# A hashed-attention kernel with a channel mix behind it: one step of the mix placed two slots later, a weight scaling placed two slots later, a flag read placed elsewhere in the program

## The chip, the cores and the metric

The kernel runs on one core of one Trainium2 chip. Its metric is the device time of one execution, in microseconds (us). Before the change it took 281.64 us (median of 3 runs, 281.24 to 282.11). A core has a matrix engine (PE, whose weight loads are listed apart as PEld), a vector engine (DVE), an activation engine (ACT), a general engine (POOL, also called GpSimd) and a sequencer that here only issues transfers (SP). Each engine works through its own instructions in program order, and waits on semaphores for the others.

## The reference

Four batches of eight heads, 768 positions and 64 features go through an attention in which a query sees only the keys of its own hash bucket. The result, 768 x 512 per batch, goes through a "channel mix":

```
mask   = q_bucket[:, :, :, None] == k_bucket[:, :, None, :]      # 6 sign bits of q@proj, k@proj
attn   = softmax(where(mask, q @ k.T / 8, -1e9));  x = attn @ v
x_prev = x shifted by one position (zero ahead of the first)
xk     = mu_k * x + (1 - mu_k) * x_prev
xr     = mu_r * x + (1 - mu_r) * x_prev
out    = sigmoid(xr @ w_r) * (relu(xk @ w_k) ** 2 @ w_v)
```

## The kernel before, in words

Two heads make a pair, four pairs make a batch, so there are 16 pairs. All of `fast()` is written in a hand-made order: the order of the Python calls is the order of the instructions on each engine. Its main loop counts slots G. Twelve slots make a turn, n = G // 12, and s = G % 12 is the slot within it. In one slot the PE makes the scores of one block of 128 keys against all 768 queries of one head (`score`, matmuls at L325), ACT takes their exponential (L332), and two slots behind it (LAG = 2) the PE multiplies them with the values (`pv`, L352). A head takes six slots, so a turn takes one pair.

Around this stand, in fixed slots of turn n:

- s = 1 (3 in turn 0), `bits`: the PE projects the queries and keys of pair n+1 (L287), DVE takes the sign bits (L291), and SP writes them in 8 small transfers (L297).
- s = 3, `turn_out`: the PE transposes the attention result of pair n-1 (L378), DVE copies it to `xt` (L379), and a copy of 127 columns (L384) completes the shifted version. That last copy is made by POOL for the first three pairs of a batch and by DVE for the fourth (t == NPB - 1).
- s = 4, `mix(..., 0)`: DVE makes df = x - x_prev (L394), then xk = mu_k * df (L398) and adds x_prev (L405). The L394 waits for the copy of L384. In turns 5 to 15, `mix(..., 1)` makes xr at s = 8 (in the first batch at odd slots of turns 4 and 5).
- s = 5, 7, 9, 11, `turn`: the PE transposes queries and keys of pair n+2 (L269), DVE copies them out of their bank (L272 for queries, L274 for keys); half goes into the operand of the scores by POOL (L277), half by DVE (L278).
- s = 6, 10, `values`: POOL converts and sums the values of pair n+1 (L305 to L315).
- s = 8, 10, `norm`: ACT squares queries and keys with a sum (L256), for pairs 6 to 15.

The matmul results lie in single banks. "A" to "D" are four of them. The attention result of a head (`oo`) takes bank A or C in turns 0 to 3, by head, and always bank A from turn 4 on (`oo_bank`, L599). The bank is free again when DVE has read it: `rc` (L363) and `ob` (L364), issued after the sixth `pv` of a head, in slot 7 for the first head of a turn. The first `pv` of the next head begins with the matmul of L343 into the same bank. It stands at the end of slot 8, after that slot's other PE work. So from turn 4 on L343 of slot 8 waits for the `ob` of slot 7.

The three products of the channel mix are a queue of items (`ffn_items`, matmuls at L424: kp, rp, vp). From turn 4 on they are issued by a credit of work per slot and fill the PE; batch b is worked on while the attention of batch b+1 runs. Their results take banks C and D in turn. A kp is read by DVE (L449) or ACT (L447) and squared by DVE (L455), an rp by ACT (L464), a vp by DVE (L487), after which SP stores the result (L491).

The weights w_v are loaded by SP in four parts (`load_wv`, L544) at s = 0 and 2 of turns 1 and 2 into two staging buffers, and POOL scales each part to bf16 (L550) eight slots after its load was issued (`later(8, ...)`). `later(k, f)` runs f at the head of the slot k after. POOL also issues the transfers of w_k and w_r (L537), w_r at s = 10 of turns 1 and 2.

At the end a flag says whether the scores stayed in a safe range (`check_bound`, L671). `nc.values_load` makes every engine read it into a register (L842), and a branch (L843) skips a slower general version. It stands after `fast()`, outside of the hand-made order; in the built program SP reads the flag ahead of its last four stores, the other engines after their last instruction.

```
                    if s == 3 and n >= 1:
                        turn_out(n - 1, mb)
                    if s == 4 and n >= 1:
                        mix((n - 1) // NPB, (n - 1) % NPB, 0)
```

Of the kernel before, what the change touches and what calls it, by code (L numbers as in the profile page):

```python
# [29 lines left out]
def kernel(  # L30
# [13 lines left out]
    nc = tc.nc  # L44
    B, H, S, D = q.shape
# [3 lines left out]
    NC_ = S // P  # L49
# [3 lines left out]
    NPB = H // 2  # L53
# [23 lines left out]
    flag = consts.tile([1, 1], INT32, name="flag")  # L77
# [90 lines left out]
    def fast():  # L168
        with ExitStack() as fx:
# [44 lines left out]
            def later(k, fn):  # L214
                due.append((clock[0] + k, len(due), fn))

            def run_due():
                ready = sorted(x[:2] for x in due if x[0] <= clock[0])
                for key in ready:
                    fn = next(x for x in due if x[:2] == key)  # L220
                    due.remove(fn)
                    fn[2]()
# [4 lines left out]
            def load_qk(n, split=False, eng=nc.sync):  # L227
                b, t = divmod(n, NPB)
                tag = f"qk{n}" if n < NKEEP else f"qk{n % 3 - 3}"
                tl = nat.tile([P, 2, 2, S // 2], FP32, name=f"qk{n}", tag=tag)  # L230
                nats[n] = tl
                if split:
                    for j in range(2):
                        for (side, i, src), e in zip(SIDES, (nc.sync, nc.scalar)):
                            e.dma_start(out=tl[:, i, j, :], in_=natural(src, b, 2 * t + j))
                else:
                    for side, i, src in SIDES:
                        eng.dma_start(
                            out=tl[:, i, :, :],
                            in_=src[b, 2 * t : 2 * t + 2].rearrange(  # L240
                                "j (p c) d -> p j (c d)", c=NC_
                            ),
                        )
# [143 lines left out]
            mx = {}  # L387
# [28 lines left out]
            def group(shape, name, mms, done):  # L416

                box = {}

                def item(i, lhs, rhs):  # L420
                    def u():
                        if i == 0:
                            box["t"] = ffbank(shape, name)
                        nc.tensor.matmul(  # L424
                            box["t"], lhs(), rhs(), start=(i == 0), stop=(i == len(mms) - 1)
                        )
                        if i == len(mms) - 1:
                            done(box["t"])

                    return u  # L430

                return [item(i, *m) for i, m in enumerate(mms)]
# [44 lines left out]
            def v_items(b, c, parts=1):  # L477
                sp, cc = divmod(c, 3)
                kcols = slice(cc * P, (cc + 1) * P)
                items = []  # L480
                w = DM // parts
                for pt_ in range(parts):
                    ms = slice(pt_ * w, (pt_ + 1) * w)

                    def done(vp, ms=ms, pt_=pt_):
                        os_ = osp.tile([P, w], FP32, name=f"os{b}_{c}_{pt_}", tag="os")
                        nc.vector.scalar_tensor_tensor(  # L487
                            out=os_, in0=mx["th", b, c][:, ms], scalar=1.0, in1=vp,
                            op0=ALU.add, op1=ALU.mult,
                        )  # L490
                        nc.sync.dma_start(  # L491
                            out=out[b].rearrange("(p c) m -> c p m", c=NC_)[c][:, ms], in_=os_
                        )

                    mms = [
                        (
                            lambda fc=fc: mx["k2", b, sp, fc][:, kcols],
                            lambda fc=fc, ms=ms: wv_sb[:, fc, ms],
                        )
                        for fc in range(NFC)  # L500
                    ]
                    items += [
                        (0.215 / parts, u)
                        for u in group([P, w], f"vp{b}_{c}_{pt_}", mms, done)
                    ]
                return items
# [35 lines left out]
            def load_wv(c0):  # L542
                st = stg.tile([P, 2, DM], FP32, name=f"wvs{c0}", tag="stg")
                nc.sync.dma_start(  # L544
                    out=st,
                    in_=moe_w_v[c0 * P : (c0 + 2) * P, :].rearrange("(c p) f -> p c f", p=P),
                )
                later(
                    8,
                    lambda: nc.gpsimd.tensor_scalar(  # L550
                        out=wv_sb[:, c0 : c0 + 2, :], in0=st, scalar1=0.5, scalar2=1.0,
                        op0=ALU.mult, op1=ALU.mult,
                    ),
                )
# [44 lines left out]
            def oo_bank(n, j):  # L599
                return "AC"[j] if n < NPB else "A"  # L600

            def misc_bank(n, s):
                return "BD"[(s // 2) % 2] if n < NPB else "B"

            for G in range(nslots + LAG):
                clock[0] = G
                n, s = divmod(G, 12)
                live = G < nslots
                run_due()

                if live and s == (5 if n == 0 else 3):
                    if n + 3 < NPAIRS:
                        load_qk(n + 3)
                    if n + 2 < NPAIRS:
                        load_v(n + 2)
                w = weights.get(n, {}).get(s)
                if w:
                    if w[0] == "v":
                        load_wv(w[1])
                    else:  # L620
                        load_w(*w)
                old = chunks[G - LAG] if G >= LAG else None
                first = old is not None and old[2] == 0
                if live:
                    score(*chunks[G])
                if old and not first:
                    pv(*old, oo_bank(*old[:2]))
                rate = 25.9 / (NPB * 12 + (3 if n >= NPAIRS - NPB else 0))
                ffn(rate / 2)
                mb = misc_bank(n, s)  # L630
                if live:
                    if n == 0:
                        if s in (0, 1):
                            turn(1, s, 1, "BD"[s])
                    if n == 1 and s == 0:
                        mups = bank(mb, [P, 2 * NDC], FP32, "mups")
                        nc.tensor.transpose(mups, mu_rows, ident32[0 : 2 * NDC, 0 : 2 * NDC])
                        nc.vector.tensor_copy(mu_sb, mups)
                    if s == (3 if n == 0 else 1) and n + 1 < NPAIRS:
                        bits(n + 1, (0, 1), mb)  # L640
                    if s == 3 and n >= 1:
                        turn_out(n - 1, mb)
                    if s == 4 and n >= 1:
                        mix((n - 1) // NPB, (n - 1) % NPB, 0)

                    if n in (NPB, NPB + 1) and G - NPB * 12 in (7, 9, 11, 13):
                        mix(0, (G - NPB * 12 - 7) // 2, 1)
                    if n > NPB and s == 8:
                        mix((n - 1) // NPB, (n - 1) % NPB, 1)
                    if s in (5, 7, 9, 11) and n + 2 < NPAIRS:  # L650
                        x = (s - 5) // 2
                        turn(n + 2, x % 2, x // 2, mb)
                    if s in (6, 10) and n + 1 < NPAIRS:
                        values(n + 1, s // 10)
                    if s in (8, 10) and NKEEP <= n + 1 < NPAIRS:
                        norm(n + 1, (s - 8) // 2)
                ffn(rate / 2)
                if old and first:
                    pv(*old, oo_bank(*old[:2]))
                if live and n >= NPB and n % NPB == 0 and s == MIXSLOT - 1:  # L660
                    queue.extend(ffn_items(n // NPB - 1))
# [16 lines left out]
            def step():  # L678
                nonlocal G
                clock[0] = G  # L680
                run_due()
                G += 1
# [14 lines left out]
            while queue:  # L697
# [7 lines left out]
                if x == 4 * NKEEP + 8:  # L705
                    check_bound()
            step()

    def general():

# [127 lines left out]
        )  # L838

    with tc.manual_schedule():  # L840
        fast()
    ok = nc.values_load(flag[0:1, 0:1], min_val=0, max_val=1)  # L842
    with tc.If(ok == 0, preferred_fallthrough_block=True):  # L843
        general()

# [29 lines left out]
```

## Time and profile before

| | |
|---|---|
| median of 3 runs | 281.64 us |
| profiled execution, its own time | 281.45 us |
| its span, first to last instruction | 279.6 us |
| mean granted PE clock | 0.988 |
| busy: PE, DVE, ACT, POOL | 94%, 71%, 77%, 41% |
| chain that ended last: PE, ACT, DVE, DMA | 66%, 9%, 8%, 7% |
| time moved by transfers | mean 107 GB/s |
| DVE L394 waited for POOL L384 | 6.9 us in 10 waits, longest 3.5 |
| POOL L550 waited for a transfer of w_v | 1.8 us, once |

A profile line such as "41.23 0.56 DVE L394 TENSOR_TENSOR df<-xt" gives the start, the duration, the engine, the line of the kernel and what is written from what. A bracket behind it is the time that the engine sat idle just before it, and what ended this. Durations of neighbours on one engine overlap by up to 0.1 us, so costs are better taken from start to start. The ends of matmuls are modelled.

### The profile page before, as it was taken

Reading aid. Unit: us, or ns where it says so; the run is one execution under the profiler, and the core shown is the slowest. Engines: PE = TensorE matmul, PEld = TensorE weight load, DVE = VectorE, ACT = ScalarE, POOL = GpSimd, SP = SyncE. Lnnn points to the kernel's source line nnn. Section 1 sums busy time; section 2 is a strip of 40 time slices with the busy share of each in tenths; the row PEclk is TensorE's granted clock in tenths of the full one; section 3 lists DMA queues with packets and bytes.
Section 4 is the critical chain, followed back from the end, with each engine's and each line's share of the span. In section 5 each row is a group of like instructions: output and inputs, shape, how many; then the busy total and the mean of one; then the engine's idle time right before and its main releaser. Section 6 shows DMA issues by size and latency. Waiting matters only on the chain.

```text
span 279.6 us, 6894 instructions
## 1 busy us (share of the span) xinstructions
PE 262.2 (94%) x2530; PEld 165.4 (59%) x2561; DVE 198.6 (71%) x438; ACT 215.0 (77%) x318; POOL 113.3 (41%) x300
## 2 busy tenths in 40 slices
PE   7999997899999999999999999999999889989991
PEld 5466765666565665656565765656565556545540
DVE  3766839879997866769698766769698835576541
ACT  2199995898799896878989896878998898449800
POOL 5885667665554350714455260715444600000000
PEclk9999997999999999999999999999999999999997
DMA  7459597253213050726122040815220001320042
GB/s 231 167 115 208 179 328 248 43 173 101 77 59 117 6 172 4 218 110 191 59 69 108 14 164 7 272 53 166 84 60 4 5 2 39 114 76 2 0 151 86
DMA packets 19896, 29.95 MB, mean 107 GB/s; under 512 B 2184, under 2 KB 15056, under 8 KB 19856
## 3 DMA queue, kind: packets, MB, share of 16 engines
q1 hardware_dynamic: 17928, 25.89, 27.9%
q0 software_dynamic: 1536, 3.15, 5.3%
q8 instruction: 22, 0.36, 0.5%
q10 hardware_dynamic: 392, 0.40, 0.5%
q14 instruction: 18, 0.15, 0.2%
HBM read 24.12 MB, written 6.29 MB: 109 GB/s over the span
## 4 chain that ended last, share of the span: by engine, by line
PE 66%; ACT 9%; DVE 8%; DMA 7%; issue 3%; SPq 3%; POOL 2%; ACTq 0%; DVEq 0%
PE sc L325 15%; PE vp L424 13%; PE kp L424 12%; PE oo L352 8%; ACT pt L332 6%; PE rp L424 5%; DMA wvs<-in_moe_w_v_dram 4%; PE bb L287 4%; PE tpq L269 3%; PE tpk L269 2%; SPq L297 2%; PE ot L378 2%; ACT sq L256 2%; PE oo L343 1%; DMA aq<-sg 1%
## 5 line engine op out<-in xcount | busy, mean ns | idle before, releaser
L332 ACT ACTIVATE pt<-sc,expb 128x768 bf16<-128x768 f32 x192 | 166.5, 904 | 39.4 <-PE sc L325 38.1
L325 PE MATMUL sc<-aq,ak 70*128 70x384 bf16 x384 | 94.9, 328 | 3.2 <-ACT pt L332 0.8
L352 PEld LDWEIGHTS <-pt 128*128 128x128 bf16 x1152 | 61.1, 98 | 26.6 <-issue 0.8
L352 PE MATMUL oo<-va,pt 128*128 128x65 bf16 x1152 | 66.9, 194 | 0.0
L424 PE MATMUL kp<-xk,wk_sb 128*128 128x384 bf16 x256 | 57.7, 325 | 0.8 <-DVE os L487 0.8
L325 PEld LDWEIGHTS <-ak 70*128 70x128 bf16 x384 | 34.9, 98 | 29.3 <-issue 9.1
L424 PE MATMUL vp<-wv_sb,k 128*128 128x512 bf16 (+1 forms) x186 | 50.3, 370 | 0.4 <-issue 0.2
L277 POOL CAST aq<-tq 64x384 bf16<-64x384 f32 x32 | 21.1, 658 | 63.3 <-DVE tq L272 63.3
L455 DVE TENSOR_TENSOR k<-kr 128x384 bf16<-128x384 bf16 x64 | 29.0, 459 | 15.5 <-ACT kr L447 14.3
L424 PEld LDWEIGHTS <-wk_sb 128*128 128x128 bf16 x256 | 22.2, 97 | 13.3 <-issue 4.2
L256 ACT ACTIVATE sq<-qk 128x768 bf16<-128x768 f32 x32 | 27.1, 847 | 0.1
L424 PE MATMUL rp<-wr_sb,xr 128*128 128x512 bf16 x79 | 24.9, 379 | 1.2 <-DVE kr L449 0.8
L424 PEld LDWEIGHTS <-k 128*128 128x128 bf16 x200 | 17.5, 97 | 12.0 <-issue 2.7
L447 ACT ACTIVATE kr<-kp 128x384 bf16<-128x384 f32 x36 | 17.7, 491 | 7.4 <-PE kp L424 7.4
L487 DVE SCALAR_TENSOR_TENSOR os<-th,vp 128x512 f32<-128x512 bf16 (+1 forms) x25 | 16.5, 663 | 9.0 <-PE vp L424 8.9
L384 POOL COPY xt<-xt 128x127 bf16<-128x127 bf16 x12 | 3.6, 302 | 46.4 <-DVE xt L379 46.4
L311 POOL TENSOR_TENSOR s<-vf 128x192 f32<-128x192 f32 x32 | 20.8, 650 | 0.0
L277 POOL CAST ak<-tk 64x384 bf16<-64x384 f32 x32 | 19.3, 602 | 2.4 <-DVE tk L274 2.4
L274 DVE TENSOR_SCALAR tk<-tpk 128x384 f32<-128x384 f32 x32 | 17.6, 550 | 3.4 <-PE tpk L269 3.3
L272 DVE COPY tq<-tpq 128x384 f32<-128x384 f32 x32 | 17.7, 552 | 2.1 <-PE tpq L269 2.0
L269 PE MATMUL tpq<-ident,qk 128*128 128x128 f32 x96 | 16.9, 287 | 2.4 <-DVE tq L272 1.7
L379 DVE COPY xt<-ot 128x768 bf16<-128x768 bf16 x16 | 8.9, 558 | 14.3 <-PE ot L378 14.2
(60 smaller groups left out, 320.0 us busy)
## 6 DMA issues: line engine op xcount, KB each, us to landing
vf<-in_v_dram SPq DMA_DIRECT2D x16, 384.0 KB
out_dram<-os SPq DMA_DIRECT2D x23, 256.0 KB
qk<-in_q_dram SPq DMA_DIRECT2D x13, 384.0 KB
qk<-in_k_dram SPq DMA_DIRECT2D x13, 384.0 KB
wvs<-in_moe_w_v_dram SPq DMA_DIRECT2D x4, 512.0 KB
aq<-sg SPq DMA_DIRECT2D x64, 4.5 KB
wk_sb<-in_moe_w_k_dram POOLq DMA_DIRECT2D x2, 512.0 KB, 5.4
ak<-sg SPq DMA_DIRECT2D x62, 4.5 KB
```

What stands on the lines that cost most here:

```text
L256: nc.scalar.activation(junk, nats[n][:, i].rearrange("p j f -> p (j f)"), AF.Square, accum_out=nrm[:, i, n : n + 1],)
L269: nc.tensor.transpose(tp[:, cols], nats[n][:, i, j, cols], ident32)
L272: nc.vector.tensor_copy(dst, tp)
L274: nc.vector.tensor_scalar(out=dst, in0=tp, scalar1=ALPHA, scalar2=None, op0=ALU.mult)
L277: nc.gpsimd.tensor_copy(au[side, j][0:D, 0:HALF], dst[0:D, :])
L311: nc.gpsimd.tensor_add(s3, vf[:, 0 : 3 * D], vf[:, 3 * D : 6 * D])
L325: nc.tensor.matmul(sc[:, sp, 0:HALF], au["k", j][:, jc * P : (jc + 1) * P], au["q", j][:, sp * HALF : (sp + 1) * HALF], start=True, stop=True,
L332: nc.scalar.activation(pt.rearrange("p (s q) -> p s q", s=2), sc[:, :, 0:HALF], AF.Exp, bias=expb, scale=SCALE,)
L352: nc.tensor.matmul(oo[:, ic, :], pts[n, j, jc][:, ic * P : (ic + 1) * P], vas[n, j][:, jc, :], start=False, stop=(jc == NC_ - 1 and ic == ...
L424: nc.tensor.matmul(box["t"], lhs(), rhs(), start=(i == 0), stop=(i == len(mms) - 1))
L447: nc.scalar.activation(kr, kp, AF.Relu)
L455: 1, lambda: nc.vector.tensor_tensor(out=k2, in0=kr, in1=kr, op=ALU.mult)
```

## The change

Three edits. For the pairs whose shifted copy is made by POOL, `mix(..., 0)` moves from slot 4 to slot 6; in turns 4, 8 and 12, and for the last pair, it stays. The scaling of a w_v part comes ten slots after the load and no longer eight. The read of the flag moves into `fast()`, between the last result and its store.

```
                            op0=ALU.add, op1=ALU.mult,
                         )
+                        if b == B - 1 and c == NC_ - 1 and pt_ == parts - 1:
+                            mx["ok"] = nc.values_load(flag[0:1, 0:1], min_val=0, max_val=1)
                         nc.sync.dma_start(
...
                 later(
-                    8,
+                    10,
                     lambda: nc.gpsimd.tensor_scalar(
...
-                    if s == 4 and n >= 1:
+                    if n >= 1 and s == (4 if n % NPB == 0 else 6):
                         mix((n - 1) // NPB, (n - 1) % NPB, 0)
...
             step()
+            return mx["ok"]
...
     with tc.manual_schedule():
-        fast()
-    ok = nc.values_load(flag[0:1, 0:1], min_val=0, max_val=1)
+        ok = fast()
     with tc.If(ok == 0, preferred_fallthrough_block=True):
```

In the built program this moves the following. On DVE, in turns 1 to 3, 5 to 7, 9 to 11, 13 and 14, the three instructions of the mix come behind the L272 and L278 of slot 5 (in turn 14, which has no turn of queries, behind an L449 and an L455) and stand directly, or with one L455 between, ahead of `rc` and `ob`. In turn 15 the order on DVE stays. On POOL parts one and three are scaled behind the query copy (L277) of slot 9, directly ahead of the transfer of w_r and the values of slot 10; parts two and four behind the key copy of slot 11, directly ahead of the next shifted copy (L383, L384). Before, the scalings stood on both sides of the query copy of slot 9. On SP the flag is read behind the last store but one and ahead of the last; before it was ahead of the last four.

More of the change, by code (lines that the diff above doesn't have):

```diff
@@ L490, in done @@
                         )
+                        if b == B - 1 and c == NC_ - 1 and pt_ == parts - 1:
+                            mx["ok"] = nc.values_load(flag[0:1, 0:1], min_val=0, max_val=1)
                         nc.sync.dma_start(
@@ L548, in load_wv @@
                 later(
-                    8,
+                    10,
                     lambda: nc.gpsimd.tensor_scalar(
@@ L642, in fast @@
                         turn_out(n - 1, mb)
-                    if s == 4 and n >= 1:
+                    if n >= 1 and s == (4 if n % NPB == 0 else 6):
                         mix((n - 1) // NPB, (n - 1) % NPB, 0)
@@ L707, in fast @@
             step()
+            return mx["ok"]
     def general():
@@ L840 @@
     with tc.manual_schedule():
-        fast()
-    ok = nc.values_load(flag[0:1, 0:1], min_val=0, max_val=1)
+        ok = fast()
     with tc.If(ok == 0, preferred_fallthrough_block=True):
```

## The prediction

> **What bounds the kernel now.** First the busy slices of the page (40 slices of 7 us, in tenths).
>
> ```profile
> PE   7999997899999999999999999999999889989991
> POOL 5885667665554350714455260715444600000000
> PEclk9999997999999999999999999999999999999997
> ```
>
> From 62 to 246 us, where the channel mix fills the PE, the table of stretches gives PE busy 179.5 of 184 us: there every wait of the PE lengthens the run. There is one dent, slices 6 and 7 (42 to 56 us), in busy time and in clock. The chain that ended last, cut to 24 to 44 us, says where it comes from (start, us, what):
>
> ```profile
> 24.17 7.82 DMA wvs<-in_moe_w_v_dram
> ...
> 32.70 4.00 DMA wvs<-in_moe_w_v_dram
> 36.78 1.04 POOL wv_sb L550
> 37.82 0.71 POOL wr_sb L537
> ...
> 41.23 0.57 DVE df L394
> ...
> 43.36 0.55 PE tpq L269 x3
> ```
>
> POOL stands at the second scaling until its transfer has landed (36.70), then works through what is queued behind it, and comes to the shifted copy at 40.91. DVE, in order, waits for that copy, and the PE for DVE. The timeline shows both waits in its brackets:
>
> ```profile
> 41.23 0.56 DVE L394 TENSOR_TENSOR df<-xt 128x768 bf16<-128x768 bf16 x1 [3.52 <-POOL xt L384]
> ...
> 43.36 0.33 PE L269 MATMUL tpq<-ident,qk 128*128 128x128 f32 x1 [1.75 <-DVE tq L272]
> ```
>
> The reader is to see that L394 isn't late for its own sake: L272 behind it frees the bank that the PE needs. The price is read from the spacing of the turns: the first L287 of turns 1 to 4 stand at 24.06, 34.62, 47.85 and 58.72. Turn 1 takes 10.56 us (ACT sets that pace), turn 2 13.23, turn 3 10.87.
>
> **Part 1, scaling and mix in turns 1 to 3: a gain.** In turn 2 the new order gives POOL: query copy of slot 9 from 33.4, scaling 1.0, w_r 0.75, values 1.9, key copy 0.5, second scaling (landed at 36.70) about 38.2 to 39.2, shifted copy about 39.5, not 40.9. DVE no longer stands there: L272 has its transposes at 38.77 and goes at 38.8, not 42.75. Both excesses could go: 13.23 - 10.56 = 2.67 and 10.87 - 10.56 = 0.31, at most 2.98. What is late next is DVE: with the mix between L278 and `rc`, the slots 6 to 11 of turns 1 to 3 run about 1.0 to 1.5 us behind, and catch up only at the `ob` of slot 1 (34.73 in turn 1); I take off 0.5. Another thing may take the stall's place: an L278 took 3.06 us at 46.85 (355 ns is its median) while POOL ran two scalings, a copy and w_r back to back. The new order splits the pair of scalings, but puts w_r directly behind one. So **-2.5**, ends -3.0 and 0. On SP, the load of part three waits for the first scaling, and would go at about 35.1, not 34.78; the eight transfers behind it wait for an L291 until 36.12 anyhow, so it costs nothing; uncovered it would be 0.3. Part four's load stands at 42.10 behind those eight, later than its scaling needs to be.
>
> **Part 2, the mix in the turns that fill the PE: a loss.** The waits of L394 there are only 0.18 to 0.39 us, and end on DVE. What matters is what the mix is moved behind and ahead of. Turn 6 on DVE and the PE, before:
>
> ```profile
> 92.36 0.56 DVE L379 COPY xt<-ot 128x768 bf16<-128x768 bf16 x1 [0.55 <-PE ot L378]
> 93.30 0.56 DVE L394 TENSOR_TENSOR df<-xt 128x768 bf16<-128x768 bf16 x1 [0.39 <-POOL xt L384]
> ...
> 95.10 0.55 DVE L272 COPY tq<-tpq 128x384 f32<-128x384 f32 x1
> ...
> 97.35 0.56 DVE L364 TENSOR_TENSOR ob<-oo,rc 128x384 bf16<-128x384 f32 x1
> ```
>
> ```profile
> 94.21 0.49 PE L269 MATMUL tpq<-ident,qk 128*128 128x128 f32 x3
> ...
> 98.21 0.33 PE L343 MATMUL oo<-vs,epsm 128*128 128x390 bf16 x1
> ```
>
> Before, the mix (1.53 us from start to start) fills DVE's time until the transposes end at 94.70. In the new order L272 comes first, so DVE has nothing to do but one L455 from 92.93 to 94.74, and the mix comes after, ahead of `rc` and `ob`. But `ob` frees bank A for L343, and was only 0.30 us ahead of it (97.91 against 98.21). New `ob` end = new start of L272 + the old stretch from L272 to the end of `ob` (2.81, less waits that fall away) + 1.53 = 94.74 + 2.81 + 1.53 = 99.08; L343 would wait 0.87. The same for each turn that moves; where an L449 or L487 stands ahead of L272, L272 starts when that one is done:
>
> | turn | L272 new | to `ob` end | `ob` end new | L343 before | wait |
> |---|---|---|---|---|---|
> | 5 | 79.25 | 2.82 | 83.60 | 82.73 | 0.87 |
> | 6 | 94.74 | 2.81 | 99.08 | 98.21 | 0.87 |
> | 7 | 110.86 | 1.74 | 114.13 | 114.02 | 0.11 |
> | 9 | 142.21 | 2.88 | 146.62 | 145.61 | 1.01 |
> | 10 | 157.67 | 1.88 | 161.08 | 161.09 | 0 |
> | 11 | 173.64 | 1.73 | 176.90 | 176.81 | 0.09 |
> | 13 | 204.07 | 3.27 | 208.87 | 207.70 | 1.17 |
> | 14 | (L449) 220.29 | 2.34 | 224.16 | 223.07 | 1.09 |
>
> Sum 5.2 us. Behind the waiting L343 on the PE's queue stands everything: `pv`, the next scores (so ACT's exponentials) and the mix's products. Waits of the PE for ACT that lie just behind (0.18 at 103.76, 0.24 at 225.97, 0.42 at 228.76) go into it: 0.84 off. So **+4.4**. Ends: 0, if DVE or the PE meets otherwise; above, two rows. The mix now lies beside POOL's copies and values, where the one of turn 14 took 2.01 us (218.17 to 220.18) and not 1.53: +0.48 in five turns is 2.4 more. And the clock, next.
>
> The wait of 1.75 us at 43.36 was followed by a granted clock of 0.55, 0.50, 0.50 and 0.74 in the microseconds from 44 to 48, which is 1.71 us of full clock lost; the wait of 0.75 at 221.18 left it at 1.00. The new waits (0.87 to 1.17) lie between and nearer to 0.75, so I count no drop; five drops would be 8.5 us. [...]
>
> [...]
>
> **Part 3, the flag: a small loss.** The title says the read goes ahead of the last store, but the rows show that on SP it was ahead of four:
>
> ```profile
> L842 SPq TENSOR_LOAD <-flag x1: 549/549/549, 268.9 to 268.9; - x1
> L842 SPq FUSED_REGOPS  x1: 192/192/192, 269.5 to 269.5; - x1
> L842 SPq SEQ_ASSERT  x1: 33/33/33, 269.8 to 269.8; - x1
> ```
>
> There it lay in SP's idle time. Now it stands between the last two stores, issued at 273.02 (0.33 long) and 273.89. From 273.39 it takes about 0.95 (268.9 to 269.85), so the last store goes at about 274.35: +0.45. Nothing covers it: SP's branch (274.6) and its next step (277.3) follow that store, and the end at 279.6 follows these. That store's issue took 0.63 where others took 0.33, and 0.3 of this may go. So **+0.4**, ends +0.15 and +0.7. On the other engines the read keeps its place.
>
> **Sum.** 281.45 (the profiled execution, 279.6 of it span) - 2.5 + 4.4 + 0.4 = 283.75, say **283.7**. The median of the runs shown is 281.64, 0.2 above that execution; I don't add it.
>
> **Rivals.** (A) The late `ob` is absorbed, and the gain of the early turns remains: 281.45 - 2.5 + 0.4 = 279.35, faster. The place is the end of slot 8. For it speaks that L343 waited for `ob` only once before (0.2 us) and that DVE is busy 140 of the 184 us there; against it, that the slack there is 0.14 to 0.8 us by the rows, while `ob` moves by 0.8 to 1.4 by the table. It decides where DVE, between slots 3 and 7, makes up about 1 us of the 1.53 that the table adds. (B) Half of it is absorbed: about 281.5, no change. (C) The early gain doesn't come, because POOL's queue or an L278 like that of 46.85 puts a new wait there: 281.45 + 4.4 + 0.4 = 286.25. (D) The new waits make the clock fall, in about half of them: 283.75 + 4.3 = 288. (E) That the edits don't do what they say is true of the flag alone, and is in the sum.
>
> **How the numbers follow.** Forecast 0.50 (its own range 282.4 to 285.2: each part's sum 0.9 off on one side, part of the 2.4 on the other), A 0.20 (278.9 to 280.3), B 0.10, C 0.12, D 0.08. The range 279.0 to 286.6 leaves out D, a quarter of A and a third of C, together 0.17. A measurement of this kernel can tell 0.3%, 0.84 us, from no change. Faster by more (under 280.8): A, 0.20. Within: B and the low edge of the forecast, 0.15. Slower (over 282.5): 0.65.
>
> **What would show it.** Right: L394 waits for POOL nowhere more than a few tenths, turn 2 takes under 11.1 us, no slice of the clock under 9 between start and end; the PE waits at L343 for `ob` about 0.9 us in turns 5, 6, 9, 13 and 14, and hardly in 7, 10, 11; SP's flag read between the last two stores, and 5.7 us again from the last store to the end. Wrong: no waits at L343 (then A), a turn 2 over 12.5 us (C), clock below 1.0 behind a wait at L343 (D).

## The result and the profile after

The changed kernel takes **288.9 us** (median of 4 runs, 288.83 to 289.10), the kernel before 281.88 us beside it (4 runs, 281.24 to 282.11): a ratio of 1.0254, 95% interval 1.0235 to 1.0273. Slower was right; the 283.7 was 5.2 us short, and the time lies above the range of 279.0 to 286.6. The profiled execution took 288.83 us, 286.9 of it span. In its listing, lines up to 490 keep their numbers and later ones are 2 higher (the scaling is L552, the store L493); the flag's read is L492. Here and below, medians and counts leave out four executions that fell into a slower state of the chip, one each of e2_scale, e3_mix, e9_after and of the kernel before beside e5 to e8.

The page's rows of busy tenths, in 40 slices of 7.2 us:

```profile
PE   7999998899989899999989999999979899989990
PEclk9999999999999999999999999999999999999996
```

The dent in the clock of slices 6 and 7 is gone, and no other took its place. The view of all waits of the PE shows what came instead:

```profile
PE oo L343 <- DVE ob L364: 8.6, 8, 1.6
```

That is 8.6 us in 8 waits, the longest 1.6, where the kernel before had one of 0.2. Where the time went can be read from the spacing of the first L287 of the turns (us):

| turn | 1 | 2 | 3 | 4 | 5 | 6 | 7 | 8 | 9 | 10 | 11 | 12 | 13 |
|---|---|---|---|---|---|---|---|---|---|---|---|---|---|
| before | 10.56 | 13.23 | 10.87 | 14.39 | 15.59 | 15.87 | 15.48 | 15.81 | 15.77 | 15.72 | 15.48 | 15.23 | 15.67 |
| after | 10.50 | 10.93 | 10.93 | 14.59 | 17.12 | 17.27 | 16.22 | 15.83 | 17.26 | 16.64 | 16.23 | 15.24 | 17.05 |

Up to turn 4 the changed kernel is 2.13 us ahead (56.59 against 58.72). Turns 4 to 13 cost 8.44 us. From turn 14 to the last L487 it is 59.59 against 59.71 us: a new wait of 1.29 us in turn 14 is made up for, since two waits of before are gone, 0.75 for an L449 (at 221.18; the mix no longer stands ahead of it on DVE) and 0.42 for ACT (at 228.76). From the start of the last L487 to the end it is 7.32 against 6.11 us. Together -2.13 + 8.44 - 0.12 + 1.20 = +7.39, the difference of the spans (286.94 and 279.55).

The chain of waits, cut to where turn 2 stood before (start, us, what):

```profile
34.80 1.03 POOL wv_sb L552
35.82 0.74 POOL wr_sb L539
...
38.95 1.02 POOL wv_sb L552
40.02 0.37 POOL xt L384
40.41 1.29 DVE df L394
```

POOL goes from a scaling to the next step and waits for no transfer; L394 waited for POOL 0.3 us in all (6.9 before). But L394 itself now takes 1.29 us. The same shows in turn 6, first DVE, then POOL, then the PE:

```profile
93.97 0.36 DVE L455 TENSOR_TENSOR k<-kr 128x384 bf16<-128x384 bf16 x1 [1.46 <-ACT kr L447]
94.40 0.56 DVE L272 COPY tq<-tpq 128x384 f32<-128x384 f32 x1
...
95.92 0.80 DVE L394 TENSOR_TENSOR df<-xt 128x768 bf16<-128x768 bf16 x1
96.75 0.63 DVE L398 TENSOR_SCALAR xk<-df,mu_sb 128x768 bf16<-128x768 bf16 x1
97.42 0.56 DVE L405 TENSOR_TENSOR xk<-xk,xt 128x768 bf16<-128x768 bf16 x1
...
98.50 0.56 DVE L364 TENSOR_TENSOR ob<-oo,rc 128x384 bf16<-128x384 f32 x1
```

```profile
95.67 0.50 POOL L305 CAST va<-vf 128x384 bf16<-128x384 f32 x1
96.11 0.12 POOL L309 MEMSET va<- 128x6 bf16 x1
96.17 0.99 POOL L311 TENSOR_TENSOR s<-vf 128x192 f32<-128x192 f32 x1
```

```profile
99.21 0.33 PE L343 MATMUL oo<-vs,epsm 128*128 128x390 bf16 x1 [1.24 <-DVE ob L364]
99.38 0.34 PE L352 MATMUL oo<-va,pt 128*128 128x65 bf16 x6
```

The order is the one that the forecast drew: L272 right behind a late L455, the mix behind it, then `ob`, then the PE. The lengths are not: from start to start the mix takes 1.97 us here (95.92 to 97.89), not 1.53. L394 begins 0.25 us before POOL's L305 is done (96.17) and takes 0.25 more than its 0.55; POOL's L311 beside it takes 0.99 us, where in turn 6 of the kernel before it took 0.79 (0.58 at its shortest). The last two rows show a second thing: the L352 starts 0.17 us behind an L343 that is listed as 0.33 long, so by these rows a PE that has waited has lost some 0.16 us more than the bracket says. Turns 5, 6, 7 and 11 each exceed their old length by their bracket and 0.16.

At the end, SP's rows for the flag and for the two stores around it:

```profile
L492 SPq TENSOR_LOAD <-flag x1: 540/540/540, 280.7 to 280.7; - x1
```

```profile
L493 SPq DMA_DIRECT2D out_dram<-os x2: 332/869/1406, 279.2 to 281.6; - x2
```

The store at 279.2 takes 1.41 us to issue, the read follows at 280.7, and the last store goes at 281.6, 1.97 us behind the last L487 (0.45 before).

### The profile page after: what moved, and what is told of

It reads as the page before. It is cut to its first block, busy times and chain, and to the rows that moved or that the text cites. A ratio compares the mean times of both kernels' runs of the same rounds, so it can differ in the third digit from the quotient of the medians.

```text
span 286.9 us, 6903 instructions
## 1 busy us (share of the span) xinstructions
PE 261.8 (91%) x2530; PEld 164.4 (57%) x2561; DVE 201.4 (70%) x438; ACT 216.5 (75%) x318; POOL 119.2 (42%) x300
## 3 DMA queue, kind: packets, MB, share of 16 engines
HBM read 24.12 MB, written 6.29 MB: 106 GB/s over the span
## 4 chain that ended last, share of the span: by engine, by line
PE 57%; DVE 21%; ACT 5%; DMA 4%; POOL 4%; issue 4%; SPq 2%; ACTq 0%; DVEq 0%
PE sc L325 12%; PE vp L424 12%; PE kp L424 11%; PE oo L352 7%; PE rp L424 4%; DVE df L394 4%; PE bb L287 4%; ACT pt L332 3%; DMA qk<-in_k_dram 3%; DVE xk L405 3%; DVE tq L272 3%; DVE xk L398 2%; DVE ob L364 2%; PE tpq L269 2%; DMA qk<-in_q_dram 2%
## 5 line engine op out<-in xcount | busy, mean ns | idle before, releaser
L325 PE MATMUL sc<-aq,ak 70*128 70x384 bf16 x384 | 93.9, 325 | 2.5 <-ACT pt L332 0.5
L352 PEld LDWEIGHTS <-pt 128*128 128x128 bf16 x1152 | 60.5, 97 | 25.6
L352 PE MATMUL oo<-va,pt 128*128 128x65 bf16 x1152 | 66.3, 193 | 0.0
L277 POOL CAST aq<-tq 64x384 bf16<-64x384 f32 x32 | 21.2, 661 | 56.3 <-DVE tq L272 56.3
L455 DVE TENSOR_TENSOR k<-kr 128x384 bf16<-128x384 bf16 x64 | 26.5, 419 | 17.7 <-ACT kr L447 16.8
L277 POOL CAST ak<-tk 64x384 bf16<-64x384 f32 x32 | 19.2, 601 | 13.0 <-DVE tk L274 13.0
L272 DVE COPY tq<-tpq 128x384 f32<-128x384 f32 x32 | 17.7, 554 | 9.8 <-PE tpq L269 9.5
L487 DVE SCALAR_TENSOR_TENSOR os<-th,vp 128x512 f32<-128x512 bf16 (+1 forms) x25 | 16.5, 663 | 9.6 <-PE vp L424 9.4
L384 POOL COPY xt<-xt 128x127 bf16<-128x127 bf16 x12 | 3.9, 324 | 45.2 <-DVE xt L379 45.2
L311 POOL TENSOR_TENSOR s<-vf 128x192 f32<-128x192 f32 x32 | 22.2, 693 | 0.0
L274 DVE TENSOR_SCALAR tk<-tpk 128x384 f32<-128x384 f32 x32 | 17.6, 548 | 2.5 <-PE tpk L269 2.5
L364 DVE TENSOR_TENSOR ob<-oo,rc 128x384 bf16<-128x384 f32 x32 | 17.8, 558 | 1.1
```

The costliest lines, as they stand in the source:

```text
L272: nc.vector.tensor_copy(dst, tp)
L274: nc.vector.tensor_scalar(out=dst, in0=tp, scalar1=ALPHA, scalar2=None, op0=ALU.mult)
L277: nc.gpsimd.tensor_copy(au[side, j][0:D, 0:HALF], dst[0:D, :])
L311: nc.gpsimd.tensor_add(s3, vf[:, 0 : 3 * D], vf[:, 3 * D : 6 * D])
L325: nc.tensor.matmul(sc[:, sp, 0:HALF], au["k", j][:, jc * P : (jc + 1) * P], au["q", j][:, sp * HALF : (sp + 1) * HALF], start=True, stop=True,
L352: nc.tensor.matmul(oo[:, ic, :], pts[n, j, jc][:, ic * P : (ic + 1) * P], vas[n, j][:, jc, :], start=False, stop=(jc == NC_ - 1 and ic == ...
```

## The experiments

Theory: the early turns gain by themselves; the loss is `ob` freeing its bank late, which the order on DVE causes and the work of POOL beside the mix makes larger; the flag adds its own length at the end. Rivals: the loss comes from the slot as such; the stretch doesn't matter; the flag costs nothing. Each ratio is against the kernel before on the same chip; e1 to e4 ran on one chip (before 282.66 us, 23 runs), e5 to e8 on another (282.66, 28 runs), e9 to e11 on a third (283.38, 11 runs).

**e1_flag**: the flag edit alone.

```
+                            mx["ok"] = nc.values_load(flag[0:1, 0:1], min_val=0, max_val=1)
                         nc.sync.dma_start(
```

> Of the three edits only the flag read, on the kernel before. After the change the last stretch (start of the last L487 to the end of the span) was 7.3 us, before it 6.2, and the store ahead of the flag read was issued in 1.41 us where other stores take 0.33. Theory 1 (the read sits on SP between the last two stores, and the store ahead of it is held as well): +1.1 us, 0.4%, with a long store issue again. Rival (the long store issue was chance of that execution, only the 0.95 us read itself counts against 0.45 of idle time): +0.4 us, no store over 0.7 us.

283.1 us (12 runs), ratio 1.0012 (0.9995 to 1.0028): +0.34 us, not told from nothing. Its profile has the end of the changed kernel: 7.54 us from the last L487, the store ahead of the read 1.54 us long. Read alone, the runs say little; see e10_noflag.

**e2_scale**: the scaling alone.

```
-                    8,
+                    10,
```

> Of the three edits only the scaling ten slots behind its load, the mix stays in slot 4. Theory 1 (both early edits work on the same stall; POOL reaches the shifted copy of turn 2 earlier, at about 39.5 and not 40.9): L394 waits about 2.1 us and not 3.5, turn 2 takes about 11.8 us and not 13.2, total -1.4 us. Rival (the gain of turn 2 is the mix's new place alone): turn 2 unchanged at 13.2, total 0. Rival (the scaling alone removes it all): turn 2 at 10.6 to 10.9, total -2.3.

279.86 us (11 runs), ratio 0.9931 (0.9900 to 0.9961): -2.8 us by the medians, -2.0 by the ratio, more than theory 1 said. Turns 1 to 3 take 10.59, 11.17 and 11.40 us; turn 2 lies between theory 1 and the second rival. L394 still waits, 1.71 us in turn 2:

```profile
39.93 0.56 DVE L394 TENSOR_TENSOR df<-xt 128x768 bf16<-128x768 bf16 x1 [1.71 <-POOL xt L384]
```

but no longer long enough to hold the PE for 1.75 us.

**e3_mix**: the mix alone.

```
-                    if s == 4 and n >= 1:
+                    if n >= 1 and s == (4 if n % NPB == 0 else 6):
```

> Of the three edits only the mix in slot 6. Theory 1 (the loss is the mix ahead of ob in the turns that fill the PE): waits of L343 for ob of 8.6 us in turns 5 to 14 as with all three edits, turn 2 at 10.6 to 11.5, total +5.5 to +6.2. Rival (the scaling edit has a part in the loss, by moving POOL's work): clearly less loss in turns 4 to 13 than the 8.4 us with all three edits.

289.75 us (4 runs), ratio 1.0267 (1.0232 to 1.0301): +7.1 us by the medians, more than expected. The waits at L343 are 1.37, 1.24, 0.58, 1.38, 0.58, 0.59, 1.46 and 1.29 us: the changed kernel's, to a tenth in all but turn 13 (1.58). The whole loss of the later turns is this edit. Turns 1 to 3 still gain (10.54, 11.63, 11.17), but less than with the scaling edit beside it.

**e4_early**: the scaling, and the mix at slot 6 in turns 1 to 3 alone.

```
+                    if n >= 1 and s == (6 if n < NPB else 4):
```

> Scaling ten slots behind and the mix in slot 6, but the latter in turns 1 to 3 alone; from turn 4 on the mix is back in slot 4, and the flag read is as before. Theory 1: the early gain alone, turn 2 at 10.9, all later turns as before: -2.3 us, 279.3 to 279.6. Rival (an earlier start of the PE-filled turns is paid back there, by transfers or ACT): -1 us or less, with turns 4 to 7 longer than before.

**280.36 us** (6 runs), ratio 0.9902 (0.9876 to 0.9928). Turns 1 to 3 take 10.69, 10.93 and 10.92 us, turns 5 to 13 what they took before. Turn 4 takes 14.94, 0.55 more than before, so the rival is right to this extent; why was not looked into. This version beats both kernels, the one before by about 1%. In turns 1 to 3 the mix alone gains 1.3 us, the scaling alone 1.5 and both together 2.1: either early edit brings most of the gain alone, so the two don't add up.

**e5_mix7**: as e4_early, but in the eight moved turns behind `ob`.

```
+                    if n >= 1 and s == (6 if n < NPB else 4 if n % NPB == 0 else 7):
```

> Scaling ten slots behind its load; the mix at slot 6 in turns 1 to 3 (as in e4_early), but in turns 5 to 7, 9 to 11, 13 and 14 at slot 7, behind rc and ob and ahead of the key copy L274. Theory (what the PE waits for decides; the mix hurts in slot 6 because ob then frees the bank late): no wait of the PE at L343 for ob in those turns, as in e4_early; but now L274 stands behind the mix and is 1.5 to 2.2 us late, and the PE waits for it at L269 of slot 9, 0.5 to 1.2 us in each of the eight turns: 4 to 8 us above e4_early (284.5 to 288.5). Rival (only ob matters on DVE in those turns): no waits of over 0.3 us at L269, time as e4_early (280.4, within 0.6).

284.12 us (10 runs), ratio 1.0046 (1.0024 to 1.0067): above e4_early by 3.8 us (medians) or 4.1 (ratios), the low end of the theory's 4 to 8. No wait at L343 is left. The PE waits for L274 instead, 0.3 to 0.73 us in turns 5, 6, 9 and 13 and 0.15 in 7 and 11, fewer and shorter waits than the theory had, and in turn 10 for an L449 queued behind the moved mix:

```profile
164.31 0.38 PE L424 MATMUL rp<-wr_sb,xr 128*128 128x512 bf16 x1 [1.21 <-DVE kr L449]
```

So the bank of `oo` was one user of DVE among several: the mix delays whoever stands behind it.

**e6_values2 and e11_values2** (the same kernel): the changed kernel with POOL's first values of a turn in slot 2, away from the mix.

```
-                    if s in (6, 10) and n + 1 < NPAIRS:
+                    if s in ((6, 10) if n < NPB else (2, 10)) and n + 1 < NPAIRS:
```

> The changed kernel, with POOL's first values of a turn (L305 to L315) in slot 2 instead of 6 from turn 4 on; the order on DVE and on the PE stays that of the changed kernel. Theory (the mix is stretched from 1.53 to some 2.2 us by what POOL does beside it): with POOL's values elsewhere the mix takes 1.55 to 1.7 us in the moved turns of 5 to 14, the waits at L343 fall from 8.6 us in all to about 4 (the forecast's table: 0.87, 0.87, 0.1, 1.0, 0, 0.1, 1.2, 1.1), and the time by 4 to 5 us against the changed kernel (284 to 285). Rival 1 (the late L272 and the order alone make the waits, the stretch is no cause): waits stay at 8 to 9 us, time as the changed kernel within 0.6 us. Rival 2 (POOL in slot 2 collides with something else): L343 waits fall but a wait of some other line takes their place, over 2 us in sum.

286.49 us (4 runs; the profiled one, of 288.29, with a late transfer in turn 3), ratio 1.0102 (1.0060 to 1.0145). L394 is back at 559 ns in the median (746 in the changed kernel), and the waits for `ob` fall from 8.6 to 4.0 us. Against the result above the gain was 2.4 us by the medians and 4.3 by the ratios, on two chips, so it ran again beside the changed kernel:

> The kernel of e6_values2 again, beside the changed kernel on the same chip, because e6_values2 gave 2.4 us less by the medians and 4.3 us less by the ratios of two calls. Theory (the stretch beside POOL is worth what turns 5 to 13 of the two profiles differ by): 2.6 us under e9_after, plus up to 0.8 for turn 14, so 2.6 to 3.4; the late order alone then keeps some 5 to 6 us of the loss. Rival (the stretch is worth the whole 8 x 0.65 us): 5 us under it.

285.85 us (6 runs), ratio 1.0111 (1.0059 to 1.0163), against 289.30 for **e9_after**, the changed kernel itself (5 runs, ratio 1.0187, 1.0138 to 1.0236, under the 1.0254 that was expected; on this chip the runs of before spread from 281.6 to 285.4):

> The changed kernel once more, as the measure for the two beside it on the same chip. Expected as before: ratio 1.0254 to the kernel before (1.0235 to 1.0273), L343 waits of 8.6 us in all.

So 3.5 us less, by the medians and by the profiled executions (285.84 and 289.3). Turn 6 of e11_values2, DVE and then the PE:

```profile
96.32 0.56 DVE L394 TENSOR_TENSOR df<-xt 128x768 bf16<-128x768 bf16 x1
96.91 0.42 DVE L398 TENSOR_SCALAR xk<-df,mu_sb 128x768 bf16<-128x768 bf16 x1
97.36 0.56 DVE L405 TENSOR_TENSOR xk<-xk,xt 128x768 bf16<-128x768 bf16 x1
```

```profile
99.04 0.33 PE L343 MATMUL oo<-vs,epsm 128*128 128x390 bf16 x1 [0.67 <-DVE ob L364]
```

With POOL's values out of its way the mix is as short as before the change in five of the eight turns, and here the wait halves. Turn by turn (us; the wait is the idle time of the PE ahead of L343 in slot 8. Those of about 0.1 are too short for the brackets of the views, which list waits from 0.15 us on. The forecast counted from start to start, so 0.16 is to be added to a measured wait to compare it):

| turn | 5 | 6 | 7 | 9 | 10 | 11 | 13 | 14 | sum |
|---|---|---|---|---|---|---|---|---|---|
| wait, forecast | 0.87 | 0.87 | 0.11 | 1.01 | 0 | 0.09 | 1.17 | 1.09 | 5.2 |
| wait, e11_values2 | 0.67 | 0.67 | 0.11 | 0.65 | 0.10 | 0.10 | 0.88 | 0.65 | 3.8 |
| wait, after | 1.37 | 1.24 | 0.58 | 1.38 | 0.58 | 0.59 | 1.58 | 1.29 | 8.6 |
| mix, e11_values2 | 1.53 | 1.52 | 1.72 | 1.51 | 1.71 | 1.71 | 1.52 | 1.52 | |
| mix, after | 2.23 | 1.97 | 2.19 | 2.12 | 2.20 | 2.20 | 2.22 | 2.04 | |

In turns 7, 10 and 11 the mix follows L278 directly, and its L394, still beside POOL's query copy (L277), takes 0.75 us. The stretch that goes with the values adds 4.8 us to these waits, 0.47 to 0.73 in each turn. What is left is nearly all the order: 3.8 and eight times 0.16 is 5.1 us, where the forecast's table has 5.2. With the values in slot 2 come waits that the changed kernel doesn't have (0.32 in turn 5, 0.49 in turn 9, 0.50 in turn 13, 1.3 in all), so the time falls by less. The rival that the order alone makes the loss is out, and so is the one that the stretch makes all of it: turns 5 to 13 remain 5.7 us above the kernel before.

**e7_mix5**: as e4_early, but one slot later in the eight turns, still ahead of slot 5's L272.

```
+                    if n >= 1 and s == (6 if n < NPB else 4 if n % NPB == 0 else 5):
```

> As e4_early, but in turns 5 to 7, 9 to 11, 13 and 14 the mix at slot 5, ahead of slot 5's L272 as before, not at slot 4. Theory (what costs is that the mix stands behind L272 and the wait for the transposes, which sends it into the time of rc and ob; not that it is late by a slot): mix 1.53 to 1.6 us, no waits at L343 over 0.3, time as e4_early (280.4, within 0.5). Rival (each slot later costs a part): waits at L343 of 0.2 to 0.5 us, 1 to 3 us above e4_early.

282.38 us (12 runs), ratio 0.9980 (0.9958 to 1.0002): 2 us above e4_early, so the expectation failed. The turns say where: 5, 7, 11 and 13 are as long as in e4_early (to 0.02), 6 is longer by 0.90, 9 by 1.14, 10 by 0.15. In turns 6 and 9 the PE waits 0.61 and 0.62 us at L343, and the slot puts the mix behind an instruction that waits:

```profile
92.75 0.36 DVE L455 TENSOR_TENSOR k<-kr 128x384 bf16<-128x384 bf16 x1 [1.46 <-ACT kr L447]
93.03 0.55 DVE L394 TENSOR_TENSOR df<-xt 128x768 bf16<-128x768 bf16 x1
...
141.04 0.56 DVE L449 TENSOR_SCALAR kr<-kp 128x384 bf16<-128x384 f32 x1 [1.54 <-PE kp L424]
141.51 0.55 DVE L394 TENSOR_TENSOR df<-xt 128x768 bf16<-128x768 bf16 x1
```

The mix could have run in those 1.5 us; now they are empty and `ob` is late. (The brackets of these two waits name POOL's L312, which ended in the same moment but makes the values of the next pair; L343 starts 0.15 us behind the end of `ob`, as in every wait for it.) In turn 14 the mix stands behind an L455 that waited 1.30 us, and L343 waits 1.27; that wait is made up for within the turns behind it, as in the changed kernel. So the theory was too narrow: not only L272 does this, the L455 of turns 6 and 14 and the L449 of turn 9 ahead of the mix do too. Being a slot later cost nothing in the four turns that are as long as in e4_early.

**e8_flagearly**: as e4_early, with the flag read right behind where it is written.

```
                 if x == 4 * NKEEP + 8:
                     check_bound()
+                mx["ok"] = nc.values_load(flag[0:1, 0:1], min_val=0, max_val=1)
```

> As e4_early, but the flag is read by all engines right behind the place where it is written, in the last turn and long ahead of the last stores. Theory (a read of the flag costs where it stands in the way of the engine that sets the end): on SP nothing at the end, tail of 5.7 to 6.3 us behind the last L487 as before; on the PE, whose read now stands ahead of products of the mix, a wait for the flag of 0.3 to 1.0 us once, so 280.6 to 281.4 (e4_early 280.4). Rival (the read frees nothing at the end and costs nothing on the way): as e4_early within 0.3. Against both: below 280.1, if the reads at the end of PE, DVE and ACT had delayed the branch.

281.1 us (12 runs), ratio 0.9942 (0.9917 to 0.9966), as the theory said: 5.73 us from the last L487 to the end, against 6.69 in e4_early, and one wait of the PE ahead of its next products, a little longer than expected:

```profile
268.38 2.96 PE L424 MATMUL vp<-wv_sb,k 128*128 128x512 bf16 x13 [1.34 <-DVE flag L671]
```

**e10_noflag**: the changed kernel without the flag edit, beside e9_after.

> The changed kernel without the flag edit: the read stands behind all of fast() again. Theory of the forecast (the read stands serially between the last two stores): 0.4 us under e9_after, as the runs of e1_flag gave (0.34, with an interval that takes in 0). Rival (what the profiles of e1_flag and of the changed kernel show, tails of 7.5 and 7.3 us against 6.1 to 6.7, holds in all executions): 1.0 us under it. Second rival (the read costs nothing): same within 0.2.

287.70 us (6 runs), ratio 1.0163 (1.0117 to 1.0208): 1.6 us under e9_after by the medians, with overlapping intervals; nearer to the rival's 1.0 than to the 0.4. Its last stores:

```profile
L491 SPq DMA_DIRECT2D out_dram<-os x3: 333/384/1072, 278.7 to 280.4; - x3
```

The long store is here too (1.07 us, begun at 279.3), but the last one follows it at 280.4, 0.7 us behind the last L487 (279.70); in e9_after it goes 2.1 us behind it. Over all profiles, the time from the last L487 to the end is 7.03 to 7.54 us, mean 7.36, in the five with the read between the last two stores, and 6.11 to 6.69, mean 6.29, in the seven with the read ahead of the last four: the flag costs about 1.07 us in profiled executions. The two comparisons by runs, 0.34 and 1.6, lie on both sides of that.

## Why the prediction was wrong

**What bounds the kernel**: right. The seven waits at L343 between turn 5 and turn 13 come to 7.32 us and these turns grew by 8.24; those of turns 5, 6, 7 and 11 each lengthened their turn by their bracket and 0.16.

**Part 1**: right. It forecast -2.5, and the turns show -2.13 up to turn 4, e4_early -2.3 by its median and -2.8 by its ratio of 0.9902. What was named as late next is what came: the PE waits 0.65 us for L274 in each of turns 2 and 3. Turn 2 takes 10.93 (under 11.1). The forecast looked no further than turn 3; turn 4 is 0.20 us longer than before in the changed kernel and 0.55 in e4_early.

**Part 2**: the mechanism was right, its size wrong: +4.4 forecast, +8.3 measured (turn 4 to the last L487; 0.2 of it in turn 4, where nothing was moved). The step that failed is the 1.53 in "the old stretch from L272 to the end of `ob` ... + 1.53". The mix takes 1.97 to 2.23 us in its new place, because POOL's copy and values, released by the same L272, run beside it. The forecast had the row for that (2.01 us in turn 14), but put it into the range, and for five turns, instead of into the sum, and for all eight: each of them stands beside the copy or the values of that slot. The waits so rose by 4.8 us where 2.4 was the end of the range. The order itself was priced well: with the mix at 1.51 to 1.72, e11_values2 delays L343 by 5.1 us in all, against the table's 5.2.

The 0.84 taken off for waits on ACT failed as well, in place and in sum. The 0.18 in turn 6 stood unchanged behind the new wait, and of the two in turn 14 only the 0.42 went; 0.27 is left of the 0.24. Yet turn 14 made up for all of its wait, more than it was credited with, because the 0.75 us for an L449 at 221.18 fell away too: there the move helped, and the forecast used that row for the clock alone. Lost overlap, about 0.16 in each of seven turns, was in the table, which worked with starts, and so is no further term.

**Part 3**: +0.4 forecast, ends 0.15 and 0.7; about 1.07 in the profiles, 1.20 in the first pair. The 0.95 of the read was right. What failed is that the store ahead of it was taken as 0.33 us long, from the one profile at hand. In ten of the twelve others it takes 1.07 to 1.62 (0.33 in e5_mix7, 0.78 in e8_flagearly). Without the read, most of that passes while the last result is still being made; with it, the read waits behind it (the last store went 0.7 us behind the last L487 in e10_noflag, 2.1 in e9_after). That the end would be 5.7 us behind the last store was near (5.3).

**Rivals**: A and B fall: only the wait of turn 14 was absorbed. C falls by turn 2. D falls: eight waits of 0.58 to 1.58 us, and the granted clock stays at 1.00 behind each. With the terms as measured, 281.45 - 2.1 + 8.3 + 1.2 = 288.85, against the 288.83 of the profiled execution.

## What to carry to other kernels

When an instruction is moved on one engine, take its duration from a row with the same neighbours on the other engines: what releases it in its new place releases others too, and those then run beside it (1.97 to 2.23 us here, where 1.53 was taken). Ask what it will be queued behind: the same step was free behind a busy engine (to 0.02 us, turns 5, 7, 11 and 13 of e7_mix5) and cost 0.90 and 1.14 us behind an instruction that waits (turns 6 and 9). A change that helps in one stage and hurts in another can be split by a condition on the stage: e4_early kept the gain of the early turns and lost nothing in turns 5 to 13.

## What the runs showed of the hardware

- **DVE and POOL stretch each other.** The three instructions of the mix take 1.53 us alone (turn 6 of the kernel before) and up to 2.46 beside POOL's work (turns 2 and 3; 2.86 in turn 3 of e9_after); L398, with one large input, goes from 420 to 619 ns in the median, and a POOL L311 takes from 0.58 to 0.99.
- **The clock fell behind the longest waits only.** Waits of the PE of 1.24 to 1.58 us (at L343 in the changed kernel) left the granted clock at 1.00. Waits of 1.75 (before), 1.79 (e1_flag) and 1.90 us (a late transfer in e6_values2) were each followed by 0.50. The drops are those of three executions: on the chip of e1 to e4, 10 of the 23 runs of the kernel before had a mean granted clock of 0.992 to 0.997, where the profiled one had 0.988, so the drop may not come each time; how long the PE waited in those was not traced. The table of stretches around the longest wait of the changed kernel (ended at 214.01), and around that of 1.90 (ended at 53.48) in e6_values2; the columns are the stretch, its length, PE busy, the granted clock, the share of the DMA engines and GB/s:

```profile
213.00:214.00 1.00, 0.00 (x0) 1.00 0.72 260
214.00:215.00 1.00, 0.99 (x15) 1.00 0.03 9
215.00:216.00 1.00, 0.95 (x9) 1.00 0.00 0
```

```profile
53.00:54.00 1.00, 0.52 (x4) 1.00 0.12 30
54.00:55.00 1.00, 1.00 (x13) 0.85 0.05 14
55.00:56.00 1.00, 1.00 (x11) 0.50 0.00 0
```

- **A store that takes 1.1 to 1.6 us to issue** where others take 0.33: the last but one, in ten of thirteen profiles, with the flag edit and without. It begins shortly ahead of DVE's read of the flag and ends behind it; in the kernel before and in e5_mix7 the last store took 0.63 and 0.72 instead. In e8_flagearly, where no engine reads the flag near it, it took 0.78. Whether the read is its cause was not settled.
